# A Fourier filter plus a gated MLP on one core: the fifth column class joins the others, column copies over two pairs, more gate/up places, a new order

## The chip, the cores and the metric

The kernel runs on one core of one Trainium2 chip. A core has a matrix engine (TensorE, PE), three engines for elementwise work (VectorE, DVE; ScalarE, ACT; GpSimd, POOL), and SyncE (SP), which here only issues transfers. Data lies in an on-chip memory with 128 partitions; matmul results land in PSUM, which the kernel uses as 8 banks of 512 fp32 values per partition. The metric is the device time of one execution in microseconds (us): the median of three runs of the kernel before is 198.14 us (198.12 to 198.24).

## The reference

`x` is 2048 x 640 in bf16. Two branches and `x` itself are added:

```python
xn = _layernorm(x, axis=-1)
# A: a filter in the frequency domain
X = rfft2(xn, axes=(-2, -1))          # 2048 x 321, complex
X = X * (w_r + 1j * w_i)
y = irfft2(X, s=(S, D), axes=(-2, -1))
# B: a gated MLP, F = 1536
h = einsum("bsd,df->bsf", xn, w_gate) * einsum("bsd,df->bsf", xn, w_up)
out = x + y + einsum("bsf,fd->bsd", h, w_down)
```

Both branches read the normalised `xn`; the kernel normalises its tile X in place, and reads `x` a second time for the final sum.

## The kernel before

**Tasks and their order.** The kernel is written as 976 small tasks. Each has a name, the engine it may run on, the data it reads and writes, and a function that issues one or a few instructions. A table `_PLAN` (lines 404 to 514) lists the tasks once more as triples of task number, engine and PSUM bank: `(24, 0, 2)` puts task 24 on PE in bank 2. `replay` takes the triples in this order, so that each engine has a fixed list, and `compute_waits` derives the semaphore waits from the data. On the chip an engine works through its own list in order; a task whose data isn't there holds up everything behind it on that engine. Engines meet only through these waits. The costs that stand in the code are used to make such a table, not at run time. Loads are issued by SP, and two of the first by ACT.

**The head.** `ld_x0a` and `ld_x0b` bring the two halves of row block 0 (a block is 128 rows), `ld_x1` to `ld_x3` blocks 1 to 3, `ld_x4` blocks 4 to 7 and `ld_x5` the last eight. `ld_gwF_0` brings two blocks of 128 columns of w_gate from column block F on, `ld_gwF_1` those of w_up (320 KB each; four blocks for F = 8). For the layernorm a block's mean and variance come from DVE (`bn`, `ag`: lines 758 and 765) or, for the blocks in `act_set` and for blocks 6 to 15, from ACT (`sm`, line 740, the mean; `sq`, line 749, the squares, each with an accumulator read). `sd` (lines 774 and 775) is the square root on ACT, `rs` and `mul` (line 799) on DVE normalise the block in place. Blocks 0 to 3 are then transposed on PE (`T0`, line 818) and copied out (`eT0`; for blocks 0 and 1 in two parts, `eT0_0_act` on ACT and `eT0_0_dve` on DVE); blocks 4 to 15 are transposed by transfers (`xt`). The transposed rows are the tile XT. While nothing else can run, PE does `warm` (line 718) and, behind the first transposes, `fill` (line 707): matmuls of ones whose result nobody reads.

**Gate and up.** `GU` multiplies 128 columns of w_gate or w_up with 128, 256 or 512 transposed rows (line 968 for 128 and 256, line 948 for 512), five matmuls over the 640 inputs. `eG` (helper lines 683 on ACT, 684 on DVE) copies the result from PSUM into one of three places in the tile GBF, and `H` on DVE (lines 984 and 985) multiplies gate and up into the tile HT. A place is free again when its `H` is done. This work, 50 units of a gate and an up, has its matmuls from 6.8 us to 133 us, in among everything else.

**Rows of the transform.** `S1` to `S5` on DVE (lines 860 to 895) and `R` on PE (line 908) make the row transform of length 640 as 2 x 5 x 64; `eR` copies it out.

**Columns of the transform, 66 to 134 us.** For each of 16 values of t: `D` (line 1025) does two frequencies' short column transforms, and its result is copied as two pieces of 64 partitions x 321 columns per frequency part (`eD`, lines 683 and 684) into a ring A of three. `C` (line 1045) does the long column transform, 321 columns for each of two frequencies. `WM` on DVE multiplies with w_r and w_i: four instructions of 256 columns (line 1062), and two of 130 (line 1068) for the fifth class of columns, 65 of the 321. For the four classes the complex product is finished on DVE for two t at a time by `SM`, a subtraction and an addition over 64 partitions x 1,024 (lines 1089 and 1090), and `JA`, `JB` make the swapped copies (lines 1097 and 1101). For the fifth class GpSimd's `NS` copies and negates (lines 1077 to 1079, into a tile Y5), and the sum is left to PE. `IA`, the inverse column transform of one of 32 frequencies, therefore has six matmuls of 64 columns: four for the four classes (line 1116, its weights read with a stride of four) and two that add up for the fifth (line 1118). `eIA` copies the result out.

**Rows back, and the output.** `I` (line 1147) and `V1` to `V5` on DVE (lines 1171 to 1204) are the inverse row transform, in groups of four, four, four, two and two blocks (`V5_0`, `V5_4`, `V5_8`, `V5_12`, `V5_14`). For each of 16 blocks `ACC` (line 1224) multiplies HT with w_down, twelve matmuls for each half of the columns, and `IV` (line 1236) adds the last step of the inverse transform to the same bank. `FINA` on ACT copies that out, `FIN` on DVE (line 1263; line 1245 for the last block) adds `x`, and `st_out` stores. The first `IV` comes at 147.9 us.

**Loads of the filter.** `ld_w` brings w_r and w_i in pieces for four frequencies at a time, behind the normalisation of block 9 or later; `ld_sm1`, `ld_fd`, `ld_tf`, `ld_ti` and `ld_g` bring tables.

The lines of the loop over an `IA` say best what its six matmuls are:

```python
for k in range(4):
    c.e.matmul(ps[:, bk, 64 * k:64 * k + 64], yl[:, k:512:4], v_ti[:, q, 0, :], start=True, stop=True)
for i in range(2):
    ins = c.e.matmul(ps[:, bk, 256:320], v_y5[:, yr, g, 128 * i:128 * i + 128], v_ti[:, q, i, :],
                     start=(i == 0), stop=(i == 1))
```

Of the kernel before, what the change touches and what calls it, by code (L numbers as in the profile page):

```python
# [255 lines left out]
def _build_tables():  # L256
    t = {}
# [24 lines left out]
    b = np.arange(64)  # L282
# [21 lines left out]
    for o in range(2):  # L304
        own = (l_ % 2 == o).astype(np.float64)
        fd[64 * o:64 * o + 64, 512:577] = e.real * own[None, :]
        fd[64 * o:64 * o + 64, 578:641] = (e.imag * own[None, :])[:, 1:64]
        gd[0:65, 512 + 64 * o:576 + 64 * o] = w.real * own[:, None]
        gd[65:128, 512 + 64 * o:576 + 64 * o] = -(w.imag * own[:, None])[1:64]
# [50 lines left out]
_NGW = 12  # L360
_LAST = ((0, 320), (320, 512), (512, 640))
# [38 lines left out]
def _d_act(n):  # L400
# [4 lines left out]
    (11, 4, -1), (12, 1, -1), (13, 4, -1), (171, 1, -1), (170, 4, -1), (8, 3, -1), (18, 2, -1), (172, 4, -1), (173, 4, -1),  # L405
    (19, 2, -1), (20, 2, -1), (27, 2, -1), (28, 2, -1), (21, 1, -1), (14, 4, -1), (22, 2, -1), (29, 2, -1), (10, 0, 0),
    (0, 3, -1), (30, 1, -1), (23, 2, -1), (24, 0, 2), (31, 2, -1), (32, 2, -1), (26, 2, -1), (25, 1, -1), (15, 4, -1),
    (9, 0, 4), (33, 0, 6), (180, 0, 5), (34, 2, -1), (174, 4, -1), (35, 2, -1), (182, 0, 4), (175, 4, -1), (192, 0, 0),
    (187, 0, 1), (181, 2, -1), (183, 2, -1), (176, 4, -1), (184, 2, -1), (185, 0, 2), (197, 0, 3), (177, 4, -1), (16, 4, -1),
    (190, 0, 6), (44, 1, -1), (37, 2, -1), (36, 2, -1), (38, 2, -1), (39, 1, -1), (188, 2, -1), (45, 1, -1), (195, 0, 7),  # L410
    (186, 2, -1), (178, 4, -1), (40, 2, -1), (41, 2, -1), (189, 2, -1), (46, 1, -1), (193, 1, -1), (179, 4, -1), (42, 0, 2),
    (47, 2, -1), (48, 2, -1), (191, 1, -1), (196, 1, -1), (200, 0, 5), (49, 0, 4), (202, 0, 1), (43, 1, -1), (1, 4, -1),
    (17, 4, -1), (194, 2, -1), (198, 1, -1), (113, 2, -1), (50, 1, -1), (199, 2, -1), (201, 1, -1), (205, 0, 0), (114, 2, -1),
    (207, 0, 6), (2, 4, -1), (203, 1, -1), (204, 2, -1), (115, 2, -1), (212, 0, 7), (206, 1, -1), (51, 2, -1), (55, 2, -1),
    (63, 1, -1), (208, 1, -1), (52, 2, -1), (64, 1, -1), (54, 2, -1), (213, 1, -1), (65, 1, -1), (116, 2, -1), (53, 2, -1),
    (56, 2, -1), (209, 2, -1), (217, 0, 2), (57, 1, -1), (210, 0, 3), (3, 4, -1), (215, 0, 4), (222, 0, 5), (211, 1, -1),
    (117, 2, -1), (120, 0, 0), (220, 0, 3), (58, 2, -1), (66, 1, -1), (4, 4, -1), (214, 2, -1), (216, 1, -1), (59, 2, -1),
    (61, 2, -1), (67, 1, -1), (218, 1, -1), (223, 1, -1), (5, 4, -1), (227, 0, 2), (121, 1, -1), (118, 0, 6), (6, 4, -1),
    (221, 1, -1), (122, 2, -1), (219, 2, -1), (123, 2, -1), (68, 2, -1), (73, 1, -1), (225, 0, 3), (232, 0, 4), (7, 4, -1),
    (228, 1, -1), (74, 1, -1), (224, 2, -1), (226, 1, -1), (124, 2, -1), (60, 4, -1), (75, 1, -1), (62, 4, -1), (76, 1, -1),  # L420
    (69, 2, -1), (230, 0, 5), (125, 2, -1), (235, 0, 0), (237, 0, 1), (77, 1, -1), (231, 1, -1), (233, 1, -1), (83, 1, -1),
    (71, 2, -1), (70, 4, -1), (126, 2, -1), (119, 1, -1), (84, 1, -1), (78, 2, -1), (236, 1, -1), (229, 2, -1), (79, 2, -1),
# [100 lines left out]
def _build(nc, A_x, A_w_r, A_w_i, B_w_gate, B_w_up, B_w_down, out, opts=None):  # L523
# [3 lines left out]
    with es:  # L527
# [406 lines left out]
        for ui, (at_, ci, ft0) in enumerate(units):  # L934
# [7 lines left out]
            for u in range(2):  # L942
                ft = ft0 + u
                if nb == 4:
# [11 lines left out]
                    def em_eg4(c, gu=gu, rr=rr, u=u):  # L956
                        return copy_on(c, v_gbf[:, rr, u, :], ps[:, bank_of(gu), :])
# [390 lines left out]
```

## Time and profile before

| quantity | value |
|---|---|
| median of the runs shown | 198.14 us (198.12 to 198.24) |
| profiled execution, first to last instruction (span) | 196.14 us |
| median less that span | 2.0 us |
| mean granted TensorE clock | 1.000 |
| first gate/up matmul starts | 6.84 us |
| last matmul ends | 193.63 us |
| DVE busy, share of the span | 90% |
| ACT busy, share of the span | 70% |
| GpSimd busy, share of the span | 14% |

The profile is one execution, so its span isn't one of the three runs' times; what lies around it (start and end of the program) adds 2.0 us here. PE is the matmul, PEld the weight load, which runs beside it. A group of instructions is written as line, engine, operation, tile written and read, partitions x elements, and count; then the busy time in us and the mean length in ns; then the idle time of the engine just ahead of it, and what ended it. A busy PE is one with matmuls in flight: their recorded lengths overlap, and a matmul's price is the distance from one start to the next (29 ns for 64 columns, about 35 where the weights are read with a stride, 136 for 320 and 216 for 512).

When the early loads landed in that execution (us; where two stand together they are gate and up):

| load | landed | load | landed |
|---|---|---|---|
| x0a | 3.09 | x3 | 9.48 |
| x1 | 4.07 | gate 4, up 4 | 10.6, 11.8 |
| up 0 | 5.18 | gate 6, up 6 | 12.8, 15.1 |
| gate 0 | 6.31 | x4 to x7 | 16.85 |
| gate 2, up 2 | 7.44, 8.54 | gate 8, up 8 | 18.7, 20.6 |
| x2 | 9.02 | x8 to x15 | 23.91 |

### The profile page before, as it was taken

What the parts mean: (1) busy time and instruction counts of PE and PEld (TensorE: products, weight loads), DVE (VectorE), ACT (ScalarE), POOL (GpSimd) and SP (SyncE); (2) the same over time, 40 slices, a digit from 0 to 9 for tenths busy, and PEclk for the clock granted to TensorE, in tenths of its full rate; (3) what the DMA queues carried; (4) which work ended last, traced back from release to release, by engine and by line L of the source; (5) the groups of instructions that cost most, each with busy time, mean ns of one, the idle gap of its engine ahead of it and who ended that gap; (6) DMA issues with size and microseconds to landing.
All of it is one profiled execution on the core that took longest, in us unless ns stands there. A gap on an engine that the chain in (4) does not pass through costs nothing.

```text
span 196.1 us, 4290 instructions
## 1 busy us (share of the span) xinstructions
PE 191.5 (98%) x1609; PEld 123.1 (63%) x1625; DVE 176.8 (90%) x392; ACT 136.7 (70%) x299; POOL 27.8 (14%) x54
## 2 busy tenths in 40 slices
PE   8999999999999999999999999999999999999995
PEld 8898645445454455556555556557777777777774
DVE  3899999999999889999899999994999999999823
ACT  3197999999957779999989999967505343333130
POOL 1000000000000004545172254460000000000000
PEclk9999999999999999999999999999999999999999
DMA  6999995426318432541451402004301334044422
GB/s 168 306 326 369 392 180 119 116 54 134 84 37 231 183 86 55 133 117 48 110 157 47 132 5 69 0 3 132 105 0 40 97 100 152 15 137 134 134 70 67
DMA packets 29667, 23.75 MB, mean 121 GB/s; under 512 B 10448, under 2 KB 27600, under 8 KB 29520
## 3 DMA queue, kind: packets, MB, share of 16 engines
q1 hardware_dynamic: 28848, 23.08, 41.6%
q10 hardware_dynamic: 800, 0.41, 0.7%
q8 instruction: 13, 0.21, 0.4%
q14 instruction: 6, 0.05, 0.1%
HBM read 18.89 MB, written 2.62 MB: 110 GB/s over the span
## 4 chain that ended last, share of the span: by engine, by line
PE 60%; DVE 19%; issue 6%; ACT 6%; SPq 4%; DMA 4%
PE ps L1224 27%; PE ps L948 21%; ACT arena L683 4%; SPq L677 4%; DMA arena<-in_A_x_dram 4%; DVE arena L984 3%; PE ps L1147 2%; DVE arena L861 2%; PE ps L1236 2%; PE ps L1025 2%; PE ps L1116 2%; PE ps L1045 2%; DVE arena L799 2%; DVE arena L860 2%; DVE arena L895 1%
## 5 line engine op out<-in xcount | busy, mean ns | idle before, releaser
L683 ACT ACTIVATE arena<-ps 128x512 bf16<-128x512 f32 (+6 forms) x243 | 117.3, 530 | 47.3 <-PE ps L1236 21.6
L948 PE MATMUL ps<-arena 128*128 128x512 bf16 x404 | 94.9, 379 | 0.9
L948 PEld LDWEIGHTS ps<-arena 128*128 128x128 bf16 x420 | 39.0, 98 | 41.1 <-ACT arena L683 0.9
L1224 PE MATMUL ps<-arena 128*128 128x320 bf16 (+2 forms) x396 | 57.2, 295 | 0.0
L1224 PEld LDWEIGHTS ps<-arena 128*128 128x128 bf16 x396 | 37.5, 98 | 13.4
L1062 DVE TENSOR_TENSOR arena<-ps,arena 128x256 bf16<-128x256 f32 x64 | 22.7, 418 | 1.4 <-PE ps L1045 1.1
L1077 POOL COPY arena<-arena 128x126 bf16<-128x126 bf16 x16 | 8.9, 556 | 104.1 <-DVE arena L1068 104.1
L984 DVE TENSOR_TENSOR arena<-arena 128x512 bf16<-128x512 bf16 x42 | 17.9, 425 | 0.5
L968 PE MATMUL ps<-arena 128*128 128x128 bf16 (+1 forms) x160 | 13.8, 246 | 0.0
L968 PEld LDWEIGHTS ps<-arena 128*128 128x128 bf16 x160 | 12.2, 98 | 1.3 <-issue 0.2
L1079 POOL TENSOR_SCALAR arena<-arena 128x130 bf16<-128x130 bf16 x16 | 11.8, 740 | 0.0
L1263 DVE TENSOR_TENSOR arena<-arena 128x640 bf16<-128x640 bf16 x15 | 7.1, 486 | 4.8 <-ACT arena L683 4.8
L740 ACT ACTIVATE arena<-arena 128x640 bf16<-128x640 bf16 x11 | 8.3, 757 | 3.6 <-DMA arena<-in_A_x_dram 3.6
L684 DVE CAST arena<-ps 64x321 bf16<-64x321 f32 (+4 forms) x16 | 8.3, 529 | 2.6 <-PE ps L1118 1.1
L1116 PEld LDWEIGHTS ps<-arena 128*128 128x128 bf16 x128 | 7.9, 120 | 3.0 <-issue 0.5
L749 ACT ACTIVATE arena<-arena 128x640 bf16<-128x640 bf16 x11 | 9.3, 844 | 0.0
L1025 PEld LDWEIGHTS ps<-arena 128*128 128x128 bf16 x160 | 7.1, 98 | 3.3 <-issue 0.2
L1116 PE MATMUL ps<-arena 128*128 128x64 bf16 x128 | 8.5, 199 | 0.0
L1068 DVE TENSOR_TENSOR arena<-ps,arena 128x130 bf16<-128x130 f32 x32 | 8.0, 295 | 0.0
L1025 PE MATMUL ps<-arena 128*128 128x64 bf16 (+1 forms) x160 | 8.0, 193 | 0.0
L860 DVE TENSOR_TENSOR arena<-arena 128x768 f32<-128x768 bf16 (+1 forms) x10 | 7.9, 792 | 0.0
L1078 POOL COPY arena<-arena 128x126 bf16<-128x126 bf16 x16 | 7.9, 495 | 0.0
(63 smaller groups left out, 201.2 us busy)
## 6 DMA issues: line engine op xcount, KB each, us to landing
arena<-in_A_x_dram SPq DMA_DIRECT2D x19, 160.0 KB, 2.6
arena<-in_A_w_r_dram SPq DMA_DIRECT2D x30, 80.2 KB, 2.2
arena<-in_A_w_i_dram SPq DMA_DIRECT2D x30, 80.2 KB, 2.2
out_dram<-arena SPq DMA_DIRECT2D x15, 160.0 KB, 1.8
arena<-in_B_w_gate_dram SPq DMA_DIRECT2D x4, 320.0 KB, 5.4
arena<-in_A_x_dram SPq DMA_DIRECT2D x1, 1280.0 KB, 10.1
arena<-c_tf SPq DMA_DIRECT2D x4, 256.0 KB, 10.3
arena<-c_ti SPq DMA_DIRECT2D x2, 512.0 KB, 5.3
```

The source lines that it names most:

```text
L683: return c.e.activation(dst, src, _ACTF.Copy)
L749: return c.e.activation(v_jk, v_x[:, b, :], _ACTF.Square, scale=-1.0, bias=v_m32[:, b:b + 1], accum_out=v_ss[:, b:b + 1])
L860: c.e.tensor_tensor(uo[:, o, :, 0:3, :], v_xb[:, b:b + nt, 0:6:2, :], v_xb[:, b:b + nt, 5:10:2, :], op)
L948: ins = c.e.matmul(ps[:, bk, :], v_gw[:, w, j, ft, :], v_xt[:, j, rows], start=(j == 0), stop=(j == 4))
L968: ins = c.e.matmul(ps[:, bk, w * n:(w + 1) * n], v_gw[:, w, j, ft, :], v_xt[:, j, rows], start=(j == 0), stop=(j == 4))
L984: return c.e.tensor_tensor(v_ht[:, ft0, rows], v_gbf[:, rr, 0, :], v_gbf[:, rr, 1, :], _OP.mult)
L1025: ins = c.e.matmul(ps[:, bk, k * 64:k * 64 + n], v_uq[:, k, t, :], v_fd[:, k * 128 + w * n: k * 128 + w * n + n], start=True, stop=True)
L1062: c.e.tensor_tensor(dst, xh, wv, _OP.mult)
L1077: c.e.tensor_copy(yg[:, :, 65:128], yg[:, :, 257:320])
L1079: return c.e.tensor_scalar(yg[:, :, 128:193], yg[:, :, 256:321], -1.0, None, _OP.mult)
L1116: c.e.matmul(ps[:, bk, 64 * k:64 * k + 64], yl[:, k:512:4], v_ti[:, q, 0, :], start=True, stop=True)
L1224: ins = c.e.matmul(ps[:, bk, 0:sl3.stop - sl3.start], v_ht[:, ft, a * 128:(a + 1) * 128], v_wd[:, ft, sl3], start=(ft == _FT_ORDER[0]), st ...
```

## The change

Seven edits come together.

1. **Fifth class on VectorE.** `WM` writes the fifth class's products with one instruction of 260 elements (in place of two of 130) into the same tile PR as the others, ahead of them in each row of now 321. `SM` works over 4 x 321 = 1,284 elements in place of 1,024. GpSimd's `NS` and the tile Y5 go. `JC` and `JD` on GpSimd copy and negate the fifth class's 63 columns of four rows (64 partitions x 252), as `JA` and `JB` do for the other columns, so `IA` has five matmuls, one per class, and waits for `JC` and `JD` as well. The table `gd` is arranged to suit.
2. **Column copies over two pairs.** `D` is a task for two t at once and fills a pair of banks; each copy `eD` is 64 partitions x 2 x 321. The ring A has four places.
3. **Five more gate/up places.** They lie in the tile XT, in the columns of row blocks 0 to 7, and serve the units of row blocks 8 to 15 once all `GU` of the first eight blocks are done.
4. **Gate or up per task.** For 128 and 256 rows a `GU` takes two column blocks of one weight; it was one column block of both.
5. **Scratch.** The tile JK, into which `sm` and `sq` write what nobody reads, moves into a part of HT that is filled late.
6. **Block 2's mean and variance on ACT** (`act_set`), and 6 matmuls in `fill` in place of 12.
7. **A new `_PLAN`.** Every engine's order is another.

By name, the first tasks of the two queues of the head:

```
before, SP:  ld_x0a ld_x1 ld_gw0_0 ld_gw2_0 ld_gw2_1 ld_x2 ld_x3 ld_gw4_0 ld_gw4_1 ld_gw6_0 ld_gw6_1 ld_x4 ld_gw8_0 ld_gw8_1 ld_sm1 ld_x5
changed, SP: ld_x0a ld_x1 ld_x2 ld_gw0_0 ld_x3 ld_gw2_0 ld_gw2_1 ld_x4 ld_gw4_1 ld_gw4_0 ld_x5 ld_sm1 ld_gw6_1 ld_gw8_1 ld_gw6_0 xt7 ld_gw8_0
before, ACT:  ld_x0b ld_gw0_1 sd_0 sd_1 eT0_0_act sm3 sd_2 sq3 sd_3
changed, ACT: ld_x0b ld_gw0_1 sd_0 sm2 sd_1 sq2 eT0_0_act sd_2 sm3 sq3 sd_3
before, PE:  warm T0_0 fill T0_1 GU_0_0 GU_1_0 GU_1_1 GU_3_0
changed, PE: warm T0_0 fill T0_1 GU_0_0_0 GU_0_0_1 T0_2 GU_0_1_0 GU_0_1_1
```

And DVE's order near the end (from the third group of the inverse rows on):

```
before:  V5_8 FIN_6 V1_12 H_48 FIN_7 V2_12 V3_12 H_49 V4_12 FIN_8 V5_12 FIN_9 eI_15 V1_14 FIN_10
changed: V5_8 FIN_6 V1_12 FIN_7 V2_12 V3_12 H_44 H_45 H_46 H_47 H_48 H_49 FIN_8 V4_12 FIN_9 V1_14 V2_14 V3_14 V5_12 FIN_10
```

The diff, without `_PLAN` and the table:

```diff
-        nfill = opts.get("nfill", 12)
+        nfill = opts.get("nfill", 6)
...
-        aset = set(opts.get("act_set", (3,))) | set(range(opts.get("act_stats", 6), 16))
+        aset = set(opts.get("act_set", (2, 3))) | set(range(opts.get("act_stats", 6), 16))
...
-        v_jk = V("JK")
+        v_jk = v_ht[:, 11, 1408:2048]
...
-            rr = ui % 3
+            late = [u_ for u_ in range(len(units)) if chunks[units[u_][1]][0] >= 8]
+            if ui in late:
+                rr = late.index(ui) % (_NG + 5)
+                rr = (rr + late[0]) % _NG if rr < _NG else rr
+            else:
+                rr = ui % _NG
+            gb = v_gbf[:, rr] if rr < _NG else v_xt[:, rr - _NG, 0:1024].rearrange("p (u n) -> p u n", u=2)
...
-                    for w in range(2):
+                    for i in range(2):
                         for j in range(5):
-                            ins = c.e.matmul(ps[:, bk, w * n:(w + 1) * n], v_gw[:, w, j, ft, :],
+                            ins = c.e.matmul(ps[:, bk, i * n:(i + 1) * n], v_gw[:, w, j, ft0 + i, :],
                                              v_xt[:, j, rows], start=(j == 0), stop=(j == 4))
...
+                    for i in range(2):
+                        for k in range(5):
+                            n = 64 if k < 4 else 65
+                            ins = c.e.matmul(ps[:, bk + i, k * 64:k * 64 + n], v_uq[:, k, t + i, :],
+                                             v_fd[:, k * 128 + w * n: k * 128 + w * n + n], start=True, stop=True)
...
+                        return copy_on(c, v_a[64 * w:64 * w + 64, ar:ar + 2, 324 * g:324 * g + 321],
+                                       ps[64 * g:64 * g + 64, bk:bk + 2, 0:321])
...
-                for w in range(2):
-                    ins = c.e.tensor_tensor(d5[w], ps[:, bk:bk + 2, 256:321], wt[:, w, :, 0:321:5], _OP.mult)
-                return ins
+                d5 = v_pr[:, :, 2 * pb:2 * pb + 2, 0:65]
+                return c.e.tensor_tensor(d5, x5, wt[:, :, :, 0:321:5], _OP.mult)
...
-            def em_ns(c, yr=yr):
-                yg = v_y5[:, yr]
-                c.e.tensor_copy(yg[:, :, 65:128], yg[:, :, 257:320])
-                c.e.tensor_copy(yg[:, :, 193:256], yg[:, :, 1:64])
-                return c.e.tensor_scalar(yg[:, :, 128:193], yg[:, :, 256:321], -1.0, None, _OP.mult)
...
-                c.e.tensor_tensor(v_l[0:64, lr, :, 0, :], pa_[0:64], pb_[64:128], _OP.subtract)
-                return c.e.tensor_tensor(v_l[64:128, lr, :, 0, :], pa_[64:128], pb_[0:64], _OP.add)
+                l_ = v_l[:, lr, 63:2623].rearrange("p (g n) -> p g n", g=4)[:, :, 0:321]
+                c.e.tensor_tensor(l_[0:64], pa_[0:64], pb_[64:128], _OP.subtract)
+                return c.e.tensor_tensor(l_[64:128], pa_[64:128], pb_[0:64], _OP.add)
...
+            for nm, five, neg, i_ in (("JA", False, False, 1), ("JB", False, True, 2), ("JC", True, False, 3), ("JD", True, True, 4)):
+                T("%s_%d" % (nm, t), "pool" if five else ("act", "dve"), {"act": 1200.0, "dve": 460.0, "pool": 1300.0},
+                  lambda c, lr=lr, five=five, neg=neg: em_j(c, lr, five, neg),
...
-                    for k in range(4):
-                        c.e.matmul(ps[:, bk, 64 * k:64 * k + 64], yl[:, k:512:4], v_ti[:, q, 0, :], start=True, stop=True)
-                    for i in range(2):
-                        ins = c.e.matmul(ps[:, bk, 256:320], v_y5[:, yr, g, 128 * i:128 * i + 128], v_ti[:, q, i, :],
-                                         start=(i == 0), stop=(i == 1))
+                    for k in range(5):
+                        yl = v_l[:, lr, o_ + 128 + k:o_ + 640:4] if k < 4 else v_l[:, lr, o_:o_ + 128]
+                        ins = c.e.matmul(ps[:, bk, 64 * k:64 * k + 64], yl, v_ti[:, q, 0, :], start=True, stop=True)
```

## Prediction

> **What bounds the kernel now.** I read the page first, then TensorE's waits, the busy time by stretches, the groups of instructions by shape, and the timeline of the first 12 us. The page's first part:
>
> ```profile
> PE 191.5 (98%) x1609; PEld 123.1 (63%) x1625; DVE 176.8 (90%) x392; ACT 136.7 (70%) x299; POOL 27.8 (14%) x54
> ```
>
> TensorE (PE) is the bound. The busy time by stretches (length; then busy us and count of PE, weight load, DVE, ACT, POOL; clock; DMA) says where it is not busy:
>
> ```profile
> 0.00:10.00 10.00, 8.81 (x116) 8.29 (x117) 5.95 (x19) 2.75 (x5) 0.58 (x6) 1.00 0.91 238
> 10.00:66.00 56.00, 55.74 (x369) 32.01 (x372) 55.57 (x123) 51.22 (x116) 0.00 (x0) 1.00 0.69 192
> 66.00:134.00 68.00, 67.18 (x633) 38.41 (x643) 62.91 (x164) 61.15 (x135) 27.23 (x48) 1.00 0.26 71
> 134.00:190.00 56.00, 55.95 (x460) 41.30 (x459) 50.76 (x85) 20.71 (x44) 0.00 (x0) 1.00 0.31 97
> 190.00:196.10 6.10, 3.85 (x42) 3.13 (x39) 1.63 (x4) 0.87 (x2) 0.00 (x0) 1.00 0.19 60
> ```
>
> Of 4.6 us without PE, 1.2 lie in the first stretch, nearly all before the first matmul of any kind, and 2.25 in the last, behind the last matmul (193.63); the three between leave 0.26 + 0.82 + 0.05 = 1.13. So from the first gate/up matmul at 6.84 us PE runs 186.8 us with about 1.1 us of waits. Everything is then two questions: when does that run start, and how long is it. The groups by shape that the change touches most (busy us, mean ns, idle before):
>
> ```profile
> L683 ACT ACTIVATE arena<-ps 64x321 bf16<-64x321 f32 x58 | 25.2, 434 | 1.7 <-PE ps L1025 0.9
> ...
> L1068 DVE TENSOR_TENSOR arena<-ps,arena 128x130 bf16<-128x130 f32 x32 | 8.0, 295 | 0.0
> ...
> L1118 PE MATMUL ps<-arena 128*128 128x64 bf16 x64 | 6.8, 193 | 0.0
> ```
>
> The start of the run, in the timeline (start, length, engine, what it waited for): ACT's rows, then two of PE and one of SP's queue.
>
> ```profile
> 1.23 0.46 ACTq L677 DMA_DIRECT2D arena<-in_B_w_up_dram  x1
> 1.78 1.28 ACT L775 ACT_TABLE_LOAD   x1 [1.78 <-POOL arena L687]
> 4.28 0.29 ACT L775 ACTIVATE arena<-arena 128x1 f32<-128x1 f32 x1 [1.22 <-DVE arena L765]
> 5.27 0.29 ACT L775 ACTIVATE arena<-arena 128x1 f32<-128x1 f32 x1 [0.70 <-DVE arena L765]
> 6.20 0.38 ACT L683 ACTIVATE arena<-ps 128x256 bf16<-128x256 bf16 x1 [0.64 <-PE ps L818]
> 9.50 0.74 ACT L740 ACTIVATE arena<-arena 128x640 bf16<-128x640 bf16 x1 [2.92 <-DMA arena<-in_A_x_dram]
> 10.15 0.19 ACT L740 ACTIVATION_READ_ACCUMULATOR arena<-arena 128x1 f32 x1
> 10.24 0.28 ACT L775 ACTIVATE arena<-arena 128x1 f32<-128x1 f32 x1
> 10.43 0.81 ACT L749 ACTIVATE arena<-arena 128x640 bf16<-128x640 bf16 x1
> ```
>
> ```profile
> 6.39 0.44 PE L818 MATMUL ps<-arena 128*128 128x128 bf16 x5
> 6.84 1.33 PE L968 MATMUL ps<-arena 128*128 128x128 bf16 x21
> ```
>
> ```profile
> 1.71 0.99 SPq L677 DMA_DIRECT2D arena<-in_B_w_gate_dram  x2
> ```
>
> The square roots of rows 0 and 1 run on ACT at 4.28 and 5.27, the first transposes' copy on ACT at 6.20, and the first gate/up matmul at 6.84. From 9.50 on come one block's mean and variance on ACT (block 3, `sm3` and `sq3` in the plan), with block 2's root between.
>
> [...] 29 ns between starts in L1025. [...] No row of before has odd rows. [...] the L1077 copy takes 0.29 us alone at 75.79 and 0.81 us at 77.53, beside L1089. [...] the gate load of SP (1.71 us, landed 4.6 us later, at 6.3) came 1.1 us behind ACT's up load (1.23 us, landed 3.9 later, at 5.1), one transfer's length. I go by the trace: order of issue.
>
> **The change part by part.**
>
> *Inverse column matmuls.* L1118 had two per frequency, the changed kernel one: 32 fewer, each 29 ns. Saves 0.93 us of PE (0.8 to 1.3, since the gaps there are 27 to 40 ns). The strided four stay.
>
> *Fills.* 6 fewer at 0.39/12 = 32 ns, 0.19 us. They are hidden by the next item.
>
> *Block 2's statistics on ACT: the head.* In the changed order ACT runs sd_0, sm2, sd_1, sq2, eT0_0_act, and sm2 waits for x2. x2 is now third in SP's queue, issued at about 1.71 us, but ACT's up load was issued at 1.23. In order of issue it lands after that: 5.18 plus 160 KB at half the 1.1 us of 320 KB, at most 5.65; its data may be in a little sooner, so 5.5. Then sm2 to sd_1 is 0.74 (9.50 to 10.24), sd_1 to sq2 0.19, sq2 to the next 0.81 (behind the accumulator read). eT0_0_act starts at 5.5 + 1.74 = 7.24 instead of 6.20: 1.04 late. Queued behind it are sd_2 and block 3; who waits is the first gate/up matmul, since it reads what eT0_0_act writes. sd_1 too is at 6.24 instead of 5.27, so mul1 and the second transposes come about 1.0 late, before 7.5, and don't set the start. The run starts at about 7.8: **+1.0 us** (0.1 if x2 lands at 4.6; 1.2 at 5.65). Nothing downstream takes it back: PE has no spare time, and later loads are only easier to meet.
>
> *Are later transfers in time?* The order is now x4–7, up4, gate4, x8–15, up6, up8, gate6, in landing steps seen in before (1.1 us per 320 KB, 1.8 per x4–7, 3.1 per x8–15): gate4 about 13.5 and gate6 about 21, against PE's need at 16 and 23. Cost 0. ACT gets 1.9 us of block 2 and four 256-column copies (1.1) more early on, but starts them 3.9 us before its old 9.50, so it is ahead in 20–50 us, where before it was full (29.84 of 30).
>
> *Column copies eD.* 64 of 64x321 become 32 of 64x642, 29 on ACT. Nearest row: ACT's 128x640 copy, 706 ns. 25.2 us becomes 29 x 0.706 = 20.5: ACT is 4.7 us lighter. Hidden: ACT is not the bound there. Three take 0.83 each on DVE. C_0 needs both first pairs: 2.0 us behind the first D, PE arrives after 2.2. Cost 0.
>
> *Multiplications WM.* L1068's two start 0.20 apart (8.0/32 = 0.25 with overlap)[...].
>
> *Sums SM.* 1,284 elements in place of 1,024: L1089's 1,024 take 687 ns and L1263's 640 take 486, so 0.52 ns each, so 0.82[...].
>
> *GpSimd.* 48 operations (27.8 us) go, 16 copies and negations of 64x252 come. From 126 elements: copy 0.29 to 0.58 alone, negation of 130 0.54 to 1.05, tripled beside DVE as seen; a pair 0.8 to 3.5 us. The new wait: IA waits for both. From SM_1's end to IA_2, PE holds 3.5 us of gate/up work in the new order; from SM_15 to IA_30 also 3.5. Cost 0 to 0.5, taken 0.
>
> *Gate/up places and order.* Products H_44 to H_49 move behind the first output blocks. DVE in the tail: six H (0.34 each) ahead of FIN_8 against two, one copy of 0.83 fewer: +0.5. Counting PE's matmuls at 136 ns (320 columns) from I_3 to each first IV and DVE's V groups as in before: V5_0 has 0.5 us to spare, V5_4 0.3, V5_8 0.45, V5_12 1.3. Cost 0; 0.3 us of error would show.
>
> *PE's waits.* 1.1 us now. By the same counting I find 0.15 at R_0, perhaps 0.25 at GU_1_4_0, 0.1 at I_1, and 1 to 3 us of room at each IA; unseen ones add. I take 0.85: **-0.25**.
>
> Sum: +1.0 - 0.93 - 0.25 = -0.2 us on a span of 196.14. The runs shown are 2.0 us above that span; I take this as unchanged: 198.14 - 0.2 = **197.9**.
>
> **Rivals.** *Head not delayed:* x2 lands with x1's step, near 4.6[...]. Then +0.1 - 0.93 - 0.25: 197.0. [...] against it gate behind up. *Slower, DVE becomes the column stage's bound:* from 66 to 134 us DVE is busy 62.9 of 68. [...] C and IA wait some 3 us in all, 201. It decides from about 1.2 us per SM half. [...] *The change does nothing:* if PE's start and its waits were set by x alone, the fewer matmuls would only lengthen waits, 198.1; against it, PE is at 55.95 of 56 in 134–190.
>
> **How the numbers follow.** A change within 0.2% (0.4 us) can't be told from none. Head delayed, waits as now: 0.52, own range 197.4 to 198.6, of it 0.20 below 197.74, 0.29 within, 0.03 above 198.54. Head not delayed: 0.20, faster. Column stage late or a further wait at the head: 0.24, of it 0.22 slower. No effect: 0.04, split evenly between same and faster. Faster 0.42, same 0.33, slower 0.25. The range leaves out the 201 end and 1 in 10 below: 196.9 to 199.1.
>
> **What would show it.** Right: ACT's L738 at about 5.5 with a DMA wait, first gate/up matmul at 7.8, 160 matmuls in IA's line, run about 185.6 us. Wrong head: ACT reads x2 before 4.8. Wrong column stage: SM over 1 us, IA waiting for GpSimd or DVE, PE under 9.5 of 10 in 70–135. Wrong tail: IV waiting for L1204's successor. A clock under 1.00 in the new gap at the head would come on top.

## The result and the profile after

The changed kernel took 199.09 us (median of 14 executions, 198.07 to 199.91), the kernel before, run beside it, 198.31 us (198.05 to 200.06). The ratio is 1.0021 with a 95% interval from 0.9998 to 1.0045: no difference that this measurement can tell from none. The forecast was 197.9, its range 196.9 to 199.1. The median is at the upper edge of that range, and what put it there is not what the forecast had there.

The 14 executions of the changed kernel fall into two groups, by the mean TensorE clock that each one records: nine with 0.991 take 198.90 to 199.91 us (median 199.55), five with 1.000 take 198.07 to 198.48 (median 198.29). A mean of 0.991 is what 3.4 us at half pace make of 197.9 us. The profiled execution is one of the nine: 199.59 us, span 197.87. It is compared here with the profile of before, span 196.14: 1.73 us more.

Not all of that shows in the times. An execution of the kernel before takes 2.15 us more than its span (median of 125, run beside the experiments), one of the changed kernel or its variants 1.73 (median of 169; none is above 1.81). So the changed kernel wins 0.4 us outside the span, and at the full clock it has the time of before with a span 0.4 us longer. Why is open.

The same part of the page, for the changed kernel, and the busy time by stretches, cut where before's was cut (length; then busy us and count of PE, weight load, DVE, ACT, POOL; clock; DMA):

```profile
PE 192.2 (97%) x1587; PEld 123.4 (62%) x1587; DVE 175.4 (89%) x364; ACT 137.9 (70%) x280; POOL 13.1 (7%) x22
```

```profile
0.00:10.00 10.00, 7.41 (x78) 7.02 (x79) 4.27 (x16) 5.79 (x14) 0.60 (x6) 0.90 0.86 256
10.00:66.00 56.00, 55.44 (x390) 32.94 (x388) 53.93 (x116) 50.03 (x111) 0.00 (x0) 0.99 0.64 148
66.00:134.00 68.00, 68.00 (x602) 37.86 (x601) 62.99 (x141) 59.84 (x109) 12.48 (x16) 1.00 0.38 104
134.00:190.00 56.00, 55.80 (x473) 41.35 (x472) 52.09 (x88) 20.66 (x45) 0.00 (x0) 1.00 0.30 92
190.00:197.90 7.90, 5.58 (x54) 4.27 (x52) 2.12 (x5) 1.57 (x4) 0.00 (x0) 1.00 0.25 83
```

The column stage, 66 to 134 us, now has no idle PE at all; before it had 0.82 us. Between 10 and 190 us PE was idle 1.13 us before and is 0.76 now. The loss lies in the first stretch (7.41 of 10 in place of 8.81, and a clock of 0.90), with smaller waits in the second and the fourth.

The head, in the timeline of ACT and then of PE (start, length, what it waited for):

```profile
5.69 0.74 ACT L738 ACTIVATE arena<-arena 128x640 bf16<-128x640 bf16 x1 [1.11 <-DMA arena<-in_A_x_dram]
...
6.42 0.28 ACT L773 ACTIVATE arena<-arena 128x1 f32<-128x1 f32 x1
6.61 0.81 ACT L747 ACTIVATE arena<-arena 128x640 bf16<-128x640 bf16 x1
...
7.42 0.36 ACT L681 ACTIVATE arena<-ps 128x256 bf16<-128x256 bf16 x1
```

```profile
5.63 0.45 PE L816 MATMUL ps<-arena 128*128 128x128 bf16 x5 [0.57 <-DVE arena L797]
5.92 0.35 PE L705 MATMUL ps<-const-bfloat16-1.0 128*128 128x64 bf16 x6
7.44 0.45 PE L816 MATMUL ps<-arena 128*128 128x128 bf16 x5 [1.17 <-DVE arena L797]
7.88 1.38 PE L974 MATMUL ps<-arena 128*128 128x128 bf16 x13
```

ACT stands still until x2 lands (5.66 us), then does the mean of block 2, the root of block 1, the squares of block 2, and only at 7.42 the copy that the first gate/up matmul reads. That matmul starts at 7.88, 1.04 us later than before. PE meanwhile has a pause of 1.17 us ahead of the second transposes. What follows on the pause is in the clock (the number after the five busy times):

```profile
7.50:8.00 0.50, 0.50 (x8) 0.37 (x9) 0.15 (x2) 0.50 (x4) 0.00 (x0) 1.00 1.20 295
8.00:8.50 0.50, 0.50 (x8) 0.50 (x7) 0.50 (x3) 0.50 (x2) 0.00 (x0) 0.59 1.33 332
8.50:11.00 2.50, 2.50 (x27) 2.50 (x25) 1.34 (x6) 2.35 (x8) 0.00 (x0) 0.50 1.04 360
11.00:11.50 0.50, 0.50 (x7) 0.50 (x6) 0.50 (x3) 0.30 (x1) 0.00 (x0) 0.50 1.20 299
11.50:12.00 0.50, 0.50 (x12) 0.50 (x10) 0.50 (x2) 0.00 (x0) 0.00 (x0) 1.00 1.26 311
```

From 8.1 to 11.5 us the granted clock is 0.50, and 128-column matmuls start 107 ns apart in place of 56. PE is "busy" all that time, so no wait shows it.

Next, SP's queue at 20 to 26 us and PE's next real wait:

```profile
22.32 1.88 SPq L804 DMA_TRANSPOSE arena<-arena  x1
24.26 0.57 SPq L675 DMA_DIRECT2D arena<-in_B_w_gate_dram  x1
```

```profile
25.68 2.75 PE L952 MATMUL ps<-arena 128*128 128x512 bf16 x12
29.00 1.25 PE L952 MATMUL ps<-arena 128*128 128x512 bf16 x5 [0.56 <-DMA arena<-in_B_w_gate_dram]
```

The gate load of column blocks 8 to 11 (`ld_gw8_0`) was issued at 24.26, since SP's queue has the transpose `xt7` ahead of it, and `xt7` waits for DVE to normalise block 7. The load landed at 28.95. By the distance between starts PE lost 0.73 us there. A smaller wait, 0.37 us at 139.4, is for rows of w_down that landed at 139.73.

The groups by shape that answer to the forecast's prices:

```profile
L681 ACT ACTIVATE arena<-ps 64x642 bf16<-64x642 f32 x29 | 20.4, 704 | 1.6 <-PE ps L1035 1.0
...
L1117 PE MATMUL ps<-arena 128*128 128x64 bf16 x160 | 8.3, 198 | 0.0
L1101 POOL TENSOR_SCALAR arena<-arena 64x252 bf16<-64x252 bf16 x8 | 7.9, 991 | 17.8 <-DVE arena L1088 17.4
...
L1074 DVE TENSOR_TENSOR arena<-ps,arena 128x260 bf16<-128x260 f32 x16 | 7.0, 435 | 0.0
L1087 DVE TENSOR_TENSOR arena<-arena 64x1284 bf16<-64x1284 bf16 x8 | 6.6, 824 | 0.3
L1088 DVE TENSOR_TENSOR arena<-arena 64x1284 bf16<-64x1284 bf16 x8 | 6.6, 822 | 0.1
...
L682 POOL COPY arena<-arena 64x252 bf16<-64x252 bf16 x8 | 4.5, 568 | 100.7 <-DVE arena L1088 100.6
```

`SM` takes 0.82 us: 260 elements more than before cost 0.137 us, 0.53 ns each (0.687 us for 1,024 before). The column copy takes 0.704 us, and GpSimd's pair 1.56 us.

**Where the 1.73 us come from**, with the starts of PE's matmuls in both traces. The run from the start of the first gate/up matmul to the start of the last matmul (at 193.63 us before, which the table ahead of the prediction calls its end) begins 1.04 us later and is 187.48 us long in place of 186.78. Of these, the half pace costs 1.51: the 128- and 256-column gate/up matmuls and the transposes among them take 15.52 us from start to start, and 14.01 in the kernel with six wide fills below, whose pace is full. The gate load costs 0.73, w_down 0.37. Without these three the run would be 184.87, or 1.91 shorter than before: 0.93 for the 32 matmuls, priced as in the forecast, and by difference 1.0 for waits that are gone. The table agrees: the two late loads are all that is left of PE's idle time between 10 and 190 us (0.56 + 0.20 of the 0.76), so before's 1.1 are gone.

### The profile page after: what moved, and what is told of

Read it like the earlier page. It is cut to its first block, busy times and chain, and to the rows that moved or that the text cites. A ratio compares the mean times of both kernels' runs of the same rounds, so it can differ in the third digit from the quotient of the medians.

```text
span 197.9 us, 4118 instructions
## 1 busy us (share of the span) xinstructions
PE 192.2 (97%) x1587; PEld 123.4 (62%) x1587; DVE 175.4 (89%) x364; ACT 137.9 (70%) x280; POOL 13.1 (7%) x22
## 4 chain that ended last, share of the span: by engine, by line
PE 84%; DMA 7%; DVE 4%; ACT 3%; SPq 1%; issue 0%
PE ps L952 44%; PE ps L1222 25%; PE ps L1117 3%; PE ps L1035 2%; DMA arena<-in_B_w_gate_dram 2%; DMA arena<-in_B_w_down_dram 2%; PE ps L1054 2%; PE ps L1234 2%; PE ps L974 2%; DMA arena<-in_A_x_dram 2%; PE ps L906 2%; PE ps L1145 1%; ACT arena L738 1%; ACT arena L681 1%; DVE arena L797 1%; PE ps L816 1%
## 5 line engine op out<-in xcount | busy, mean ns | idle before, releaser
L681 ACT ACTIVATE arena<-ps 128x512 bf16<-128x512 f32 (+6 forms) x217 | 113.3, 579 | 50.8 <-PE ps L1234 18.0
L952 PE MATMUL ps<-arena 128*128 128x512 bf16 x420 | 97.4, 379 | 0.6 <-DMA arena<-in_B_w_gate_dram 0.6
L1222 PE MATMUL ps<-arena 128*128 128x320 bf16 (+2 forms) x396 | 57.1, 295 | 0.2 <-DMA arena<-in_B_w_down_dram 0.2
L974 PE MATMUL ps<-arena 128*128 128x128 bf16 (+1 forms) x160 | 15.3, 262 | 0.0
L682 POOL COPY arena<-arena 64x252 bf16<-64x252 bf16 x8 | 4.5, 568 | 100.7 <-DVE arena L1088 100.6
L747 ACT ACTIVATE arena<-arena 128x640 bf16<-128x640 bf16 x12 | 10.0, 836 | 0.1
L738 ACT ACTIVATE arena<-arena 128x640 bf16<-128x640 bf16 x12 | 8.9, 744 | 1.2 <-DMA arena<-in_A_x_dram 1.1
L682 DVE CAST arena<-ps 128x320 bf16<-128x320 f32 (+3 forms) x11 | 7.0, 662 | 2.3 <-PE ps L1117 1.4
L1101 POOL TENSOR_SCALAR arena<-arena 64x252 bf16<-64x252 bf16 x8 | 7.9, 991 | 17.8 <-DVE arena L1088 17.4
L1234 PE MATMUL ps<-arena 128*128 128x320 bf16 (+2 forms) x33 | 7.8, 295 | 0.0
L1035 PE MATMUL ps<-arena 128*128 128x64 bf16 (+1 forms) x160 | 7.0, 193 | 0.0
L1074 DVE TENSOR_TENSOR arena<-ps,arena 128x260 bf16<-128x260 f32 x16 | 7.0, 435 | 0.0
```

What stands on the lines that cost most here:

```text
L681: return c.e.activation(dst, src, _ACTF.Copy)
L682: return c.e.tensor_copy(dst, src)
L738: return c.e.activation(v_jk, v_x[:, b, :], _ACTF.Copy, scale=1.0 / _D, accum_out=v_m32[:, b:b + 1])
L747: return c.e.activation(v_jk, v_x[:, b, :], _ACTF.Square, scale=-1.0, bias=v_m32[:, b:b + 1], accum_out=v_ss[:, b:b + 1])
L952: ins = c.e.matmul(ps[:, bk, :], v_gw[:, w, j, ft, :], v_xt[:, j, rows], start=(j == 0), stop=(j == 4))
L974: ins = c.e.matmul(ps[:, bk, i * n:(i + 1) * n], v_gw[:, w, j, ft0 + i, :], v_xt[:, j, rows], start=(j == 0), stop=(j == 4))
```

## The experiments

Three theories stood after the result. **H**: the head (late start, pause, low clock) is the loss. **G**: the late gate load sets the time, so that whatever the head wins is lost again at 28 us. And the forecast's own terms, the 32 matmuls and the cover of GpSimd's copies, were still to be shown. In the plan the tasks of the head have the numbers 21 `sd_0`, 30 `sd_1`, 36 `sm2`, 37 `sq2`, 25 `eT0_0_act`; 71 is `xt7` and 177 `ld_gw8_0`.

### ACT's order at the head

```diff
-(21, 1, -1), (36, 1, -1), (22, 2, -1), (29, 2, -1), (30, 1, -1),
+(21, 1, -1), (22, 2, -1), (29, 2, -1), (30, 1, -1), (36, 1, -1),
...
-(37, 1, -1), (25, 1, -1),
+(25, 1, -1), (37, 1, -1),
```

> The changed kernel with ACT's order at the head sd_0, sd_1, sm2, eT0_0_act, sq2 in place of sd_0, sm2, sd_1, sq2, eT0_0_act. Theory H (ACT's wait for x2 delays the first gate/up matmul by 1.0 us and leaves PE idle for 1.3 us, after which the granted clock is 0.50 for 3.4 us, worth 1.7 us): first gate/up matmul at 6.9, clock 1.000 in every execution, then 0.3 us of a new wait of T0_2; span 197.9 - 1.0 - 1.7 + 0.3 = 195.5, if the gate load of column blocks 8 to 11 comes earlier by the same time, since its issue hangs on work that PE feeds. Theory G (that load, issued behind a transpose that waits for DVE, lands at 28.9 whatever PE does): the gain comes back as a longer wait at 28 us, span 197.2 to 197.9. A rival in which the head is not the cause at all: 197.9 and clock 0.991.

Measured: 198.31 us (197.47 to 199.01), ratio 0.9987 (0.9968 to 1.0006); the clock was 1.000 in all 14 executions. The first gate/up matmul started at 7.05. So ACT's order is shown to be the cause of the late start and of the low clock, but the gain over the full-clock executions of the changed kernel (198.29) is nothing. PE's timeline says what took the earlier start:

```profile
7.05 1.28 PE L974 MATMUL ps<-arena 128*128 128x128 bf16 x20
8.89 0.45 PE L816 MATMUL ps<-arena 128*128 128x128 bf16 x5 [0.56 <-DVE arena L797]
```

The transposes of block 2 come third in PE's list, and block 2's rows are normalised only by 8.9 us: 0.72 us of wait from start to start, for which the expectation had 0.3. Further on, the gate load cost 0.83 and w_down 0.52. The span was 196.6 in the median: of 197.9 - 195.5 = 2.4 us expected by H, 1.3 came, and G's 197.2 to 197.9 didn't come either.

### The gate load ahead of the transpose

```diff
-(78, 2, -1), (71, 4, -1), (177, 4, -1),
+(78, 2, -1), (177, 4, -1), (71, 4, -1),
```

> The changed kernel with the gate load of column blocks 8 to 11 issued ahead of the transpose of block 7 (two neighbours on SP's queue change places), so at about 14 us in place of 24.3. If that load is the cause of PE's wait of 0.73 us at 28.05: the wait goes, span 197.2 at clock 0.991 and 0.7 us or more less at clock 1.000, where PE arrives earlier and waits longer. If something else is late just behind it (a free gate/up place, block 4 to 7's transposes): no gain, 197.9.

Measured: 198.97 us (197.31 to 199.24), ratio 1.0017 (1.0003 to 1.0032). The load was issued at 13.97 and landed at 23.62, and the wait at 28 us is gone; the profiled span is 197.2, as expected. 18 of 21 executions had the clock of 0.991, with a median of 199.00 in place of 199.55: 0.55 us gained at the same clock. In the profiled one the clock was low from 7.7 to 11.1 us, again 3.4 us long.

### Both

> Both edits. Theory H with its own price and the load's wait apart: 197.9 - 1.0 - 1.7 + 0.3 - 0.73 = 194.8. Theory G: the same 194.8, but with the root order alone giving less than 1 us. If the gain at the head comes back as another wait before 60 us: over 196.5.

Measured: 197.52 us (197.21 to 198.09), ratio 0.9955 (0.9941 to 0.9968), faster than the kernel before by 0.45%. Together the two edits win 1.6 us of the changed kernel's median. Of the 0.8 us won over the kernel before, about half lies in the span (195.8 in the median against 196.2) and half outside it. At the full clock the root order is worth nothing (198.29 to 198.31) and the gate load 0.8 (198.31 to 197.52); what the root order gives is the clock. So H holds for the clock and falls for the start. G holds for the load's own wait, but the load isn't what takes back the earlier start: with the load early that start still buys nothing, since two of the three full-clock executions with the gate load alone took 197.3 (the third 198.68). The span was expected at 194.8 and came at 195.8 in the median. The profiled execution, span 196.4, is the slowest of its 14 (198.09 us), and it shows a thing that the mean clock, 1.000, doesn't:

```profile
6.12 0.71 PE L816 MATMUL ps<-arena 128*128 128x128 bf16 x5 [0.85 <-DVE arena L797]
6.63 0.53 PE L705 MATMUL ps<-const-bfloat16-1.0 128*128 128x64 bf16 x6
6.97 0.72 PE L816 MATMUL ps<-arena 128*128 128x128 bf16 x5
7.48 2.34 PE L974 MATMUL ps<-arena 128*128 128x128 bf16 x20
```

Five transposes take 0.72 us in place of 0.45, twenty matmuls 2.34 in place of 1.28. Their starts are 107 ns apart up to 10.15 us, then 56. The trace holds no clock record before 10.14 us, as it holds none before 5.88 in the kernel before, whose matmuls of ones are 107 ns apart up to there as well. A stretch without a record counts as 1.00, in the tables by stretches and in the mean of an execution, so a long slow start doesn't show in either.

The pause of 0.85 us ahead of the first transposes doesn't explain this by itself. After a pause of 1.00 us in the kernel with the gate load alone, and of 0.91 in the one with wide fills (below), five of them take 0.45 us. With the gate load alone PE had come to the full pace before the pause, and here it hadn't: the last twelve matmuls of ones ahead of it take 1.08 us there and 1.48 here.

What goes with the clock in these traces is how much PE works ahead of the fall. In the 3.41 us before it, as long as the stretch at half pace, PE had 1.67 us of work in the changed kernel (4.67 to 8.09) and 1.27 with the gate load alone (4.24 to 7.65). No fall follows a stretch of that length with 2.43 us of work (the root order alone, 5.48 to 8.89), with 2.88 (48 fills, below, 4.69 to 8.10) or with 3.05 (before, 3.43 to 6.84). The length of the waits alone doesn't order the cases: the transposes of the changed kernel wait 1.74 us in all, those of the kernel with GpSimd's copies doubled (below) 2.0, and that profile's clock is 1.000. Where between 1.67 and 2.43 us a limit lies, if it is the work that counts, is not shown.

### The clock alone, twice

First with many narrow fills, then with six wide ones. Both keep PE at work on ones through the pause; the first issues 42 instructions more, the second none.

```diff
-        nfill = opts.get("nfill", 6)
+        nfill = opts.get("nfill", 48)
```

> The changed kernel with 48 fill matmuls in place of 6, so that PE works on ones until 7.4 us, when the second block's transposes can start; nothing else is moved. If PE's pause of 1.3 us is what lowers the granted clock: clock 1.000 in every execution, the first gate/up matmul still at 7.9, and 0 to 1.7 us saved: span 196.2 where nothing waits longer, 196.3 to 196.8 as in the executions of the changed kernel that had the full clock. If the clock falls for another reason (the load on the chip, the transfers): 0.991 in as many executions as before, 197.9. If the fills delay the second transposes: first gate/up matmul later than 8.0.

```diff
-                ins = c.e.matmul(ps[:, bk, 64 * (i % 4):64 * (i % 4) + 64], v_one, v_one[:, 0:64], start=True,
-                                 stop=True)
+                ins = c.e.matmul(ps[:, bk, :], v_one, v_one[:, 0:1].to_broadcast([128, 512]), start=True,
+                                 stop=True)
```

> The changed kernel with its 6 fills 512 columns wide, nothing else. The clock alone: full in all executions. Against 199.09, where two thirds of the executions had the low clock: 198.1 to 198.3, the time of those that had the full clock, since the gate load lands at about 28 us whatever PE does and takes back part of the 1.7 us. If the pace is worth its whole 1.7 us: 197.8 or less. If the fills hold up the second transposes: first gate/up matmul later than 8.0, over 198.5.

Measured: with 48 fills 199.14 us (198.08 to 200.58), ratio 1.0036 (1.0021 to 1.0051); with six wide ones 198.24 us (197.81 to 199.94), ratio 0.9998 (0.9985 to 1.0010). In both the clock was 0.999 or 1.000 in all 21 executions, so it is PE's pause, and not the load on the chip, that goes with the low clock. PE with six wide fills:

```profile
5.95 0.45 PE L816 MATMUL ps<-arena 128*128 128x128 bf16 x5 [0.91 <-DVE arena L797]
6.24 1.47 PE L705 MATMUL ps<-const-bfloat16-1.0 128*128 128x512 bf16 x6
7.72 0.45 PE L816 MATMUL ps<-arena 128*128 128x128 bf16 x5
8.17 1.28 PE L974 MATMUL ps<-arena 128*128 128x128 bf16 x20
```

With wide fills the time is that of the changed kernel's full-clock executions, as expected, so the low clock costs 1.3 us of an execution (199.55 to 198.24), less than the 1.51 that it takes from PE, since the gate load takes more (0.94 us at 26.8).

The 0.9 us between the two fills were no part of any theory. The profile with 48 fills has a wait of 0.96 us at 160.7 that the other hasn't; the same pair of fills with the gate load early shows what it is.

### Late start with full pace, with and without more instructions

Both have the gate load ahead of the transpose and ACT's order as in the changed kernel.

> The changed kernel with 48 fills and with the gate load ahead of the transpose, the head's order as in the changed kernel: first gate/up matmul late (7.9 to 8.1), full pace from there, and no wait for that load. If 1 us of late start is 1 us of time: 197.5 + 0.7 to 1.0 = 198.2 to 198.5. If a late start costs nothing while the pace is full, because the next waits take it up: 197.3 to 197.6, as the three executions of the kernel with the gate load alone that had the full clock.

> The changed kernel with the gate load ahead of the transpose, and its 6 fills 512 columns wide in place of 64 (6 x 0.216 = 1.3 us, so PE works on ones until 7.2 us, with no instruction more). The first gate/up matmul is as late as in the changed kernel, the pace full. If the 1.2 us wait at 160 us in the kernel with 48 fills came from the fetch of more instructions: it is gone, 198.26 - 1.2 = 197.1, the late start then costs nothing against the 197.5 of the kernel with both edits, since that one waits 0.7 us for block 2 at 8.1 us. If the late start costs 0.7 to 1.0: 198.2 to 198.5.

Measured: 48 fills 198.26 us (197.79 to 199.21), ratio 0.9999 (0.9982 to 1.0016); six wide fills 197.53 us (197.35 to 198.07, five executions), ratio 0.9960 (0.9947 to 0.9973).

The second answers the question of the late start. Its first gate/up matmul starts at 8.18, its run is 185.13 us long, and its time is that of the kernel with both edits (197.52), whose order at the head starts at 7.05 to 7.48 in five profiles; so is 198.24 with wide fills alone against 198.31 with the root order alone. Once block 2's statistics are on ACT, a start up to a microsecond earlier is given back, because PE then waits 0.72 us for the rows of block 2. So the +1.0 us at the head is not a price that stands by itself. The 197.1 of the expectation didn't come. And the 198.26 of the first is the number expected if a late start cost 0.7 to 1.0 us, but not for that reason.

The first of the two waits 1.2 us at 160 us. Its chain there:

```profile
155.83 4.55 DMA out_dram<-arena
160.40 0.45 ACT arena L681
160.84 0.05 issue
160.89 0.31 PE ps L1222
```

The store of row block 3 takes 4.55 us to land. ACT waits for it before it copies the next result into that place, and PE waits for the bank that ACT frees. With wide fills the same store, issued at 156.14, lands at 158.72. What else the DMA engines had in that time, by queue (packets, MB, share of 16 engines), in the kernel with 48 fills from 157 to 158 us, and then in the one with wide fills from 161 to 162 us:

```profile
q1 hardware_dynamic: 211, 0.24, 83.2%
q8 instruction: 1, 0.02, 11.4%
```

```profile
q1 hardware_dynamic: 262, 0.30, 89.3%
q8 instruction: 1, 0.02, 6.3%
```

One packet of instructions is fetched about then in every variant of the changed kernel. In the three with 32 or 42 more PE instructions (48 fills, 48 fills with the gate load, and the sixth matmul below) it falls between 157 and 159 us, just when the store is under way, and the store lands 4.0 to 4.6 us after its issue. In the nine others, the changed kernel itself among them, it falls at 161 us or later, and the store lands after 2.5 to 2.6. Later the two sides change places. A store issued at 176 to 178 us has a packet beside it in the nine and lands after 3.2 to 4.4 us, and in the three it has none and lands after 2.3 to 2.4; one issued near 190 has a packet in the three (2.9 to 3.7 us) and none in the nine (1.8). That the packet delays the store, and not only keeps it company, is an inference from twelve traces; the packet was not moved by itself. Nor does it delay every store: in the kernel before, one packet starts 0.2 us after the issue of a store at 156.29 and one 1.5 us after the issue at 187.28, and they land after 2.4 and 1.8 us; with 48 fills one issued at 172.56 has a packet 1.4 us later and lands after 1.8.

### The price of a matmul in the column stage, twice

```diff
+                    ins = c.e.matmul(ps[:, bk, 256:320], yl, v_ti[:, q, 0, :], start=True, stop=True)
                     return ins
```

> The kernel with both edits and a sixth matmul in each inverse column transform: the fifth one twice, into the same place, so nothing changes but PE's work, 32 matmuls of 64 columns. If PE is what sets the time in the column stage, as the prediction has it: 197.52 + 0.93 = 198.45 (up to 198.65 at 35 ns each). If the waits take it up: 197.5 to 197.8.

```diff
-                        ins = c.e.matmul(ps[:, bk, 64 * k:64 * k + 64], yl, v_ti[:, q, 0, :], start=True, stop=True)
+                        w_ = 64 if k < 4 else 128
+                        ins = c.e.matmul(ps[:, bk, 64 * k:64 * k + w_], yl,
+                                         v_ti[:, q].rearrange("p c n -> p (c n)")[:, 0:w_], start=True, stop=True)
```

> The kernel with both edits, and the fifth matmul of each inverse column transform 128 columns wide in place of 64, the other 64 into a part of the bank that nobody reads: 32 x 64 columns more on PE [...] and not one instruction more. If PE's work counts in full and the rest of the 1.8 us that the sixth matmul cost came from its 32 more instructions (their fetch falls beside the store of row block 3, which then lands 2 us late): 197.5 + 0.85 = 198.35, and the store lands in 2.5 us. If the work itself costs twice its length: 199.2.

Measured: the sixth matmul 199.35 us (198.96 to 200.83), ratio 1.0055 (1.0038 to 1.0072), which is 1.8 us over the kernel with both edits and not 0.93. Its trace has PE waits of 0.68 us at 160.7 (the store again) and 0.88 at 193.9 (behind the store near 190 that lands after 3.7 us) that the base has not. The wider matmul, with no instruction more: 198.43 us (197.97 to 198.87), ratio 0.9996 (0.9983 to 1.0009), 0.91 us over the base, for 0.85 expected (an estimate: 32 times 26.7 ns, from the distances of 29 ns for 64 columns and 216 for 512), and its store of row block 3 landed after 2.57 us. By the two ratios it is 0.8 us, each with an interval of 0.3 us to either side. So PE's work in this stage counts in full within that error, and the change's 32 matmuls are worth about what they last.

### GpSimd's copies done twice

```diff
+                xx = arena[:, total - 504 + 252 * lr:total - 252 + 252 * lr].rearrange("p (g n) -> p g n", g=4)
+                if five and not neg:
+                    copy_on(c, xx[0:64], src[64:128])
...
+                if five:
+                    c.e.tensor_scalar(xx[64:128], src[0:64], -1.0, None, _OP.mult)
```

> The kernel with both edits and each fifth-class copy and negation on GpSimd done twice, the first time into a scratch place: a pair takes 3.0 us in place of 1.5. If the pair is hidden behind 3.5 us of gate/up work, as the prediction has it: 197.5, within 0.2. If the inverse column transforms wait for GpSimd: up to 8 x 1.5 = 12 us more in all[...].

Measured: 197.30 us (197.09 to 197.96, eight executions), ratio 0.9944 (0.9924 to 0.9964). GpSimd works 2.9 us a pair and nothing is longer: the copies are hidden with at least 1.4 us to spare, and DVE's instructions beside them keep their length (the 256 columns of `WM` 0.415 us and `SM` 0.82, as in the changed kernel).

### The waits that were left

To the kernel with both edits: `nwarm` 11 in place of 10; on PE the transposes of block 2 behind the gate/up matmuls of block 1, and on DVE `rs_2`, `mul2` behind the copies of block 1; and the load of w_down's rows 0 and 1 ahead of rows 2 and 3.

```diff
-        nwarm = opts.get("nwarm", 10)
+        nwarm = opts.get("nwarm", 11)
...
-(39, 2, -1), (34, 2, -1), (40, 2, -1), (35, 2, -1),
+(34, 2, -1), (35, 2, -1), (39, 2, -1), (40, 2, -1),
...
-(41, 0, 7), (42, 1, -1), (189, 0, 6), (191, 0, 2),
+(189, 0, 6), (191, 0, 2), (41, 0, 7), (42, 1, -1),
...
-(685, 4, -1), (684, 4, -1),
+(684, 4, -1), (685, 4, -1),
```

> The kernel with both edits (root order, gate load ahead of the transpose), and three more: TensorE's warm-up has 44 matmuls in place of 40, so that the pause ahead of the first transposes shrinks by 0.4 us; on PE and DVE the work of block 1 stands ahead of that of block 2, which waited 0.72 us at 8.1 in the run with the root order alone; and of the last loads of w_down the rows 0 and 1, which PE needs first, come before rows 2 and 3 (0.2 to 0.5 us of wait at 138). Theory (what the head and the loads cost adds up on PE): 197.52 - 0.7 - 0.3 = 196.5, and no execution with the slow pace up to 10 us. Rival (another engine sets the end by now, DVE or the stores): 197.3 to 197.5.

Measured: 197.31 us (197.09 to 197.71, nine executions), ratio 0.9944 (0.9927 to 0.9962): 0.2 us better than both edits alone, not 1.0, and as the rival had it. The profile has 56 ns from the first transposes on. None of the nine took over 197.71 us, where the slow start above took 198.09, but times alone don't show that it was in none. But a wait of 0.71 us for a transpose is at 10.0 us in place of 8.1, and w_down's rows still cost 0.45 us at 137.3. At the head the wait moved on to the next transposes; the loads' order wasn't the cause of w_down's wait (0.22 us in the profile of both edits). This kernel beats both the one before and the changed one; the kernel with GpSimd's work doubled has the same time, so the three edits beyond the first two are not shown to be worth anything.

## Why the prediction was right or wrong

The forecast of the median, 197.9, missed by 1.2 us. That the change can hardly be told from none came true, but the forecast gave this 0.33, and 0.42 to faster. In its own terms the step that failed is the length of PE's run, about 185.6 us forecast and 187.48 in the profiled execution. The 1.9 us are 1.51 of low clock and 1.10 of two late loads, both of which stood at nothing in the sum, less 0.75 that the old waits gave beyond the 0.25 (by difference). And the 2.0 us outside the span, "I take this as unchanged", became 1.7. That the median stayed near the forecast is luck in part: these errors partly cancel, and five of 14 executions were spared the low clock, without which the median would be that of the nine, 199.55.

- **The head's delay.** Right to 0.2 us in each step: x2 landed at 5.66 (5.5, at most 5.65, forecast, though 5.18 and half of 1.1 make 5.73), ACT's L738 began at 5.69, `eT0_0_act` at 7.42 (7.24), the first gate/up matmul at 7.88 (7.8). x2, issued 0.48 us after ACT's up load on the other queue, landed 0.47 us after it, as by order of issue, and gate 0 another 1.1 us later. As a price it was mis-stated: "nothing downstream takes it back" is wrong where block 2's rows are next in PE's list, as the kernel with the gate load and wide fills shows, which starts at 8.18 and loses nothing by it.
- **The clock.** This is the largest term that the sum left out. The forecast had the clock in its last sentence, "would come on top", and in no sum. It costs 1.51 us of PE in the profile, and 1.3 us of an execution, in nine of 14. In the profile two pauses of 0.57 and 1.17 us stand ahead of the fall, with 1.67 us of work in the 3.41 us up to it. Why the other five executions were spared no run here shows; an earlier landing of x2 is one possibility.
- **"Are later transfers in time? Cost 0."** Wrong, by an omission: the list named gate 4 and gate 6 (forecast at about 21, landed at 21.57) and left out gate 8, which SP holds behind `xt7`, and the rows of w_down (0.37 us). Gate 8 cost 0.73 us, and 0.8 to 0.9 where PE is on time. Fixing it won 0.55 us at the low clock and 0.8 at the full one.
- **The 32 matmuls, -0.93.** Right, within the error: 32 matmuls of the same weights, widened by 64 columns, cost 0.8 to 0.9 us for 0.85.
- **PE's waits, -0.25.** The old waits nearly all went, 1.0 us of 1.1, and two new ones came, 0.73 and 0.37: +0.1 net. The forecast took too little for the first and saw nothing of the second.
- **SM, WM, eD.** SM 0.82 us (0.82 forecast), eD on ACT 0.704 (0.706), WM's one instruction 0.435, where before's two took 0.50; what the forecast had for it was the author's estimate. The rival "DVE becomes the column stage's bound" fell: SM stayed under the 1.2 us from which it was to decide, and PE is busy for 68.00 of the stage's 68.00 us. The 201 of that rival was the author's estimate too; nothing in the traces showed so slow an SM.
- **GpSimd, cost 0.** Right; a pair takes 1.56 us, in the range of 0.8 to 3.5, and doubled it still costs nothing. The forecast took 0.29 us as GpSimd's copy alone and 0.81 beside DVE; but at 75.79 DVE was at work too, on L1062, which reads one of its operands from PSUM, while L1089 at 77.50 reads both from the on-chip memory. So it isn't any work of DVE that goes with slow copies.
- **Outside the span, 2.0 unchanged.** Mis-sized: 1.7, and 2.15 for the kernel before.
- **The tail.** No wait of `IV` in the profiled execution. But the store behind it has so little room that a landing 2 us late stops PE, which the forecast's counting of DVE and PE alone couldn't show.

## What to carry to other kernels

Follow every transfer on a queue to its issue, not to its place in the list: a load behind a transpose that waits for an engine is issued when that engine is done, here at 24.26 us and without the transpose ahead of it at 13.97. Where PE is near 100% busy, read its pace (here 107 ns from start to start in place of 56) as well as its busy time, and count pauses at the head by the clock that follows them; here six wide dummy matmuls kept it at no cost that the times show. Where a probe adds work, make instructions wider in place of adding more where that can be done: 32 and 42 more went with stores that landed 2 us late far away. And a number that an expectation named is no proof of its reason: 198.26 came from a late store and not from a late start.

## What the runs showed of the hardware

- Two PE pauses of 0.57 and 1.17 us by the profile, with 1.67 us of work in the 3.41 us up to the fall, were followed by a clock of 0.50 for 3.41 us. The mean clock that this makes, 0.991, is in nine of 14 executions of the changed kernel and in 18 of 21 with the gate load ahead. In ten kernels with the pause filled or shortened, 134 executions in all, no mean was under 0.999.
- In the 3.41 us ahead of the fall PE had 1.67 us of work in one profile and 1.27 in another; no fall followed 2.43, 2.88 and 3.05 us of work in stretches of that length in three others.
- No clock record stands before 10.14 us in the profile of the kernel with both edits, nor before 5.88 in that of before, and such a stretch counts as 1.00: matmuls started 107 ns apart up to 10.15 us in the first of the two, whose mean clock is 1.000.
- A fetch of 0.02 MB of instructions beside a store goes with a landing about 1 to 2 us late at three places of the program, in whichever of the twelve kernels it falls there (158, 177 and 190 us); at least three other stores with a fetch beside them weren't late.
- The time outside the span differs between programs: 2.15 us for the kernel before, 1.73 for the changed one and its variants.
